# An attention and expert kernel whose instruction order is planned anew with other planner numbers

## The chip, the cores and the metric

The kernel runs on one core of one Trainium2 chip. The metric is the time of one execution on the device in microseconds (us); of several runs the median is taken. Engines: PE is the matrix engine, DVE the vector engine, ACT the scalar engine, POOL the GpSimd engine, and SP issues the transfers.

## The reference

```python
q_pool = q.reshape(B, H, S // 2, 2, D).mean(axis=3)          # B 4, H 8, S 1152, D 64
scores = np.matmul(q_pool, k.transpose(0, 1, 3, 2)) / np.sqrt(D)
scores = scores - np.max(scores, axis=-1, keepdims=True)
attn = np.exp(scores)
attn = attn / (np.sum(attn, axis=-1, keepdims=True) + 1e-09)
x = np.matmul(attn, v)                 # then to (2304, 512): heads side by side
h = x @ w_in                           # 512 -> 2048
g = np.where(h > 0.0, h, np.exp(np.minimum(h, 0.0)) - 1.0)
out = g @ w_out                        # 2048 -> 512
```

All inputs and the output are float32.

## The kernel before

The work is cut into tasks, each a few instructions of one engine. A planner, the class `Plan`, puts all tasks into one list when the program is built, and the engines get their instructions in the order of that list. Each engine works through its own queue in order; semaphores hold an instruction until what it reads is written. So nothing is decided on the chip: a task that stands too early in a queue makes its engine wait, and everything behind it too.

Attention. There are four units (one for each batch) of four head pairs each. A head pair has nine steps: eight of 128 pooled queries of one head, and one that holds the last 64 queries of both heads. That is 144 steps. A step is: `scores` on PE (L814, L819, L826: six matmuls, or twelve in the ninth step) into the one PSUM tile `s`; `biggest` on DVE (L832), which scales the scores into the SBUF tile `ep` and finds the row maximum; `expo` on ACT (L838) with the row sums; `recip` on DVE (L846 or L484, L847). As there is one tile `s`, the next step's scores wait until `biggest` has read the last ones. Then there are two ways, by `SPLIT`:
- in the six pairs marked f, `norm` (L850 on POOL, L853 on DVE, or L856 on ACT), transposes on PE (L906), copies out of PSUM (L916 on ACT or L919 on DVE), and float32 matmuls with v (`pv`, L938);
- in the ten pairs marked s, the probabilities are split into two float16 parts: `phi` (L874 on POOL or L877 on ACT) writes the high part `hb`, `plo` on DVE (L880) the rest; SP transposes both by DMA (L886), and PE multiplies them with a split v (`pv_split`, L950, 54 matmuls).

The result is copied to `x` (L959 on ACT, L963 or L965 on DVE). Ahead of each pair, q and k (and v where it is split) are loaded, summed (`q_sum`, L587 on POOL or DVE), scaled and split in `prep`, and turned by DMA.

Experts. When the x of a unit's first 256 tokens, and then of its last 320, is there, `experts` runs for that group: `m1` (L1053) into PSUM, `neg` (L1066) and `ex` (L1069) on ACT, `em` (L1074) on POOL, `join` (L1079) on DVE, then `gh` (L1093 on ACT or L1101 on POOL) and `gl` (L1097 on POOL or L1105 on DVE), which make the two float16 parts of g, then `m2` (L1124) and the way out (L1140 to L1150). The weights are unpacked on DVE (L696 to L700), and split by `w_hi` on ACT (L742) and `w_lo` (L745 on DVE, or L484 and L751 on POOL).

What sets the order: each task has a key, worked out from its place in the sum of steps, from the numbers in `CFG`, and from a number of its own in `NUDGE`. In `Plan.run` a modelled engine that is free takes, of the tasks whose predecessors are done by the model's durations (`add`'s second argument) and lags (`LAT`, `TAIL`, `SWITCH`), the one with the lowest key whose buffers are free. A task with more than one way (`ways`) goes to the engine at which the model thinks it is done sooner.

PE has its array whole ("full"), or cut into row or column halves ("row", "col"): `scores` ends in "row" (or starts in "col"), `pv`, `pv_split` and the 64 token blocks of `m2` are "col", the rest is "full". `modes` says so for each task.

Of the kernel before, what the change touches and what calls it, by code (L numbers as in the profile page):

```python
# [18 lines left out]
CFG = dict(  # L19
    LOADS=-2465884, WI0=-27823, WIT=30440, WO0=1311932, WOT=4783, T0=1480, T1=812, M0=21242,  # L20
    M1=58392, KS=5164412, KM=-16195, KE=597808, KH=-20226, KL=126077, KV=-42119, KN=-15967,
    KX=-43605, KO=-36554, PEN=-18129, W0L=26355, WIN=-42633, PD=3605, KS0=29075649, KM0=3580,
    KE0=43169, KH0=-7128, KL0=17190, KV0=-37362, KX0=35076, PLM0=0, NS0=36, PLM=0, M2=6438, DP=0,
    FK=0, PENW=-13844, PENH=10146, FL=2000, PH0=2, PH=1, KT=140078, KT0=-327, LV=15492, PENN=-24464,
    PENT=-48259, PLP=1, WLP=1, HIP=0, PA=9244, PB=93473, KA=40989, KB=-4257737, KC=34460,
)
# [46 lines left out]
    "turn0": -32562, "w_hii": -11591, "w_hio": 455, "w_loi": 299, "w_loo": -451, "wi_mino": -21137,  # L73
# [48 lines left out]
class Plan:  # L122
# [4 lines left out]
    TAIL = {"PE": 70.0, "DVE": 75.0, "ACT": 90.0, "POOL": 30.0, "DMA": 0.0}  # L127
# [12 lines left out]
    def add(self, eng, dur, key, emit, after=(), bufs=(), ways=(), modes=None):  # L140
        t = Task(eng, dur, key, emit, after, list(bufs))
        for e, d, f in ways:
            t.ways[e] = (d, f)
        for b in t.bufs:
            b.open += 1
        t.modes = modes or t.modes
        t.kind = emit.__name__ + self.at
        t.key += NUDGE.get(t.kind, 0)
        t.n = len(self.tasks)
        self.tasks.append(t)  # L150
        return t
# [25 lines left out]
    def run(self):  # L177
# [33 lines left out]
        def finish(t, at):  # L211
            t.end = at
            for b in t.bufs:
                b.open -= 1
            for kid in t.kids:
                kid.left -= 1
                kid.ready = max(kid.ready, at + self.TAIL[t.eng] + (30.0 if t.eng == "DMA" else self.LAT[kid.eng]))
                if kid.left == 0:
                    heapq.heappush(coming, (kid.ready, kid.n, kid))
# [5 lines left out]
        while done < len(self.tasks):  # L225
# [5 lines left out]
            while again:  # L231
                again = False
                for e in engines:
# [3 lines left out]
                    for _, _, t in wait[e]:  # L237
                        if e != t.eng:
# [12 lines left out]
                        if need is not None:  # L251
                            best = (t, need)
                            break
# [58 lines left out]
        self.span = now  # L312
# [12 lines left out]
def attention_moe_kernel(  # L325
# [67 lines left out]
    def dve(n):  # L393
        return Port(1.08 * n + 75.0)
# [4 lines left out]
    def pol(n):  # L399
        return 0.93 * n + 150.0  # L400

    def pol2(n):
        return Port(1.9 * n + 190.0)
# [87 lines left out]
    def across(src, n, key, after, bufs, take):  # L491
# [19 lines left out]
        return plan.add("DVE", Port(600.0), key, across_take, [t3], [xp] + bufs)  # L511


    def prep(pr, t0, t1):
# [40 lines left out]
        def halves(n, kh, kl, dst_h, dst_l, src, j, after, bufs):  # L555
# [3 lines left out]
            t = plan.add("DVE", dve(n), kl, f, [h], bufs, [("POOL", Port(pol(n), pol2(n)), g)] if CFG["PLP"] else [])  # L559
# [33 lines left out]
        qa = plan.add("DVE", dve(n), key[0], qadd(nc.vector), [tq], [q32], [("POOL", pol2(n), qadd(nc.gpsimd))])  # L593
# [602 lines left out]
```

## Time and profile before

| | us |
|---|---|
| median of 3 runs (841.58 to 841.83) | 841.66 |
| profiled execution, its own time | 844.75 |
| span of the profile | 843.0 |
| PE busy in the span | 750.6 (89%) |
| DVE busy | 682.2 (81%) |
| ACT busy | 594.3 (71%) |
| POOL busy | 329.3 (39%) |

The span runs from the first instruction to the last one's end; 1.75 us of the profiled execution lie around it. "Busy" is time in which the engine has at least one instruction at work. An idle time is named by what ended it: `PE s L814 <- DVE ep L832` is PE's wait to write scores until `biggest` on DVE has read the tile.

### The profile page before, as it was taken

Reading aid. Unit: us, or ns where it says so; the run is one execution under the profiler, and the core shown is the slowest. Engines: PE = TensorE matmul, PEld = TensorE weight load, DVE = VectorE, ACT = ScalarE, POOL = GpSimd, SP = SyncE. Lnnn points to the kernel's source line nnn. Section 1 sums busy time; section 2 is a strip of 40 time slices with the busy share of each in tenths; the row PEclk is TensorE's granted clock in tenths of the full one; section 3 lists DMA queues with packets and bytes.
Section 4 is the critical chain, followed back from the end, with each engine's and each line's share of the span. In section 5 each row is a group of like instructions: output and inputs, shape, how many; then the busy total and the mean of one; then the engine's idle time right before and its main releaser. Section 6 shows DMA issues by size and latency. Waiting matters only on the chain. (4 is left out here: it accounts for less than half of the span.)

```text
span 843.0 us, 19849 instructions
## 1 busy us (share of the span) xinstructions
PE 750.6 (89%) x7821; PEld 493.3 (59%) x7821; DVE 682.2 (81%) x1352; ACT 594.3 (71%) x1024; POOL 329.3 (39%) x318
## 2 busy tenths in 40 slices
PE   0178887899899999999978989999999999999997
PEld 0036665677655675576754557566746566586553
DVE  6889989999889789978987889979988799865140
ACT  3478989888887676767867678768878687655250
POOL 2412244326688216023643128315615365235120
PEclk9999999999999999999989999999999999999999
DMA  8954576546458329794979999999999989950000
GB/s 295 242 151 124 145 182 192 177 88 149 88 109 154 78 62 219 115 181 93 205 145 198 182 184 206 143 208 213 194 190 192 200 143 163 187 94 2 25 2 31
DMA packets 310813, 125.43 MB, mean 149 GB/s; under 512 B 272576, under 2 KB 291008, under 8 KB 310720
## 3 DMA queue, kind: packets, MB, share of 16 engines
q1 hardware_dynamic: 310720, 124.16, 71.9%
q8 instruction: 61, 1.00, 0.5%
q14 instruction: 32, 0.26, 0.1%
HBM read 45.09 MB, written 4.72 MB: 59 GB/s over the span
## 5 line engine op out<-in xcount | busy, mean ns | idle before, releaser
L838 ACT ACTIVATE ep<-ep,wk 128x1152 f32<-128x1152 f32 x144 | 180.3, 1252 | 73.2 <-DVE ep L832 54.0
L832 DVE TENSOR_SCALAR_CACHE_REDUCE ep<-s,sm 128x1152 f32<-128x1152 f32 x144 | 203.2, 1411 | 27.0 <-DMA pT<-ep 11.5
L1053 PE MATMUL r<-x,wi 128*128 128x256 f16 (+1 forms) x1536 | 201.6, 289 | 5.5 <-ACT x L959 2.4
L1053 PEld LDWEIGHTS <-wi 128*128 128x128 f16 x1536 | 148.6, 99 | 50.5 <-issue 11.4
L1124 PE MATMUL r<-wo,g 128*128 128x512 f16 (+1 forms) x864 | 174.0, 380 | 0.0
L880 DVE SCALAR_TENSOR_TENSOR ep<-ep,wk,hb 128x1152 f16<-128x1152 f32 x90 | 136.0, 1518 | 6.8 <-POOL hb L874 5.1
L814 PE MATMUL s<-kT,qT 128*128 128x512 f16 (+2 forms) x480 | 98.3, 338 | 34.0 <-DVE ep L832 28.3
L1124 PEld LDWEIGHTS <-g 128*128 128x128 f16 (+1 forms) x864 | 74.1, 100 | 83.8 <-issue 4.4
L874 POOL TENSOR_SCALAR hb<-ep,wk 128x1152 f16<-128x1152 f32 x41 | 56.0, 1365 | 149.8 <-DVE wk L847 72.6
L1074 POOL TENSOR_SCALAR tmp<-tmp,us 128x320 f32<-128x320 f32 (+1 forms) x96 | 78.2, 815 | 83.9 <-ACT tmp L1069 82.4
L850 POOL TENSOR_SCALAR ep<-ep,wk 128x1152 f32<-128x1152 f32 x34 | 42.4, 1247 | 114.7 <-DVE wk L847 30.6
L877 ACT ACTIVATE hb<-ep,wk 128x1152 f16<-128x1152 f32 x49 | 61.4, 1252 | 32.0 <-issue 8.2
L814 PEld LDWEIGHTS <-qT 128*128 128x128 f16 (+1 forms) x480 | 39.8, 102 | 74.3 <-issue 36.1
L1079 DVE SCALAR_TENSOR_TENSOR tmp<-r,wk,tmp 128x320 f32<-128x320 f32 (+1 forms) x96 | 57.1, 609 | 31.6 <-POOL tmp L1074 31.4
L950 PE MATMUL r<-pT,v 128*64 128x128 f16 (+1 forms) x2700 | 79.0, 215 | 2.9 <-DVE tmp L1079 1.0
L950 PEld LDWEIGHTS <-v 128*64 128x64 f16 x2700 | 71.9, 110 | 14.2 <-issue 12.5
L906 PE MATMUL r<-ident,ep 128*128 128x128 f32 x486 | 70.5, 292 | 3.2 <-ACT ep L856 2.4
L1097 POOL TENSOR_TENSOR g<-tmp,g 128x320 f16<-128x320 f32 (+1 forms) x49 | 55.8, 1143 | 25.1 <-ACT g L1093 24.1
L906 PEld LDWEIGHTS r<-ident,ep 128*128 128x128 f32 x486 | 55.1, 147 | 17.3 <-issue 9.9
L938 PE MATMUL r<-pT,v 128*64 128x128 f32 (+1 forms) x1080 | 61.0, 268 | 1.8 <-ACT pT L916 1.7
L1066 ACT ACTIVATE tmp<-r 128x320 f32<-128x320 f32 (+1 forms) x96 | 45.8, 480 | 23.0 <-PE r L1053 20.3
L916 ACT ACTIVATE pT<-r 128x384 f32<-128x384 f32 x125 | 53.7, 489 | 10.7 <-PE r L906 9.5
(119 smaller groups left out, 1001.5 us busy)
## 6 DMA issues: line engine op xcount, KB each, us to landing
k<-in_k_dram SPq DMA_DIRECT2D x16, 576.0 KB, 4.1
v<-in_v_dram SPq DMA_DIRECT2D x16, 576.0 KB, 4.7
q<-in_q_dram SPq DMA_DIRECT2D x32, 256.0 KB, 3.7
g<-in_moe_w_out_dram SPq DMA_DIRECT2D x14, 512.0 KB, 4.5
qT<-qT SPq DMA_DIRECT2D x48, 144.0 KB, 2.8
g<-in_moe_w_in_dram SPq DMA_DIRECT2D x13, 512.0 KB, 6.0
out_dram<-tmp SPq DMA_DIRECT2D x16, 256.0 KB, 2.7
h<-in_moe_w_in_dram SPq DMA_DIRECT2D x3, 512.0 KB, 3.8
```

The source lines that it names most:

```text
L814: nc.tensor.matmul(s.ap[rows, c, 0:n], pr.qT.ap[:, 0, j, rows], keys[h][c], start=True, stop=False, skip_group_check=True,)
L832: nc.vector.tensor_scalar(e_(), s.ap.rearrange("p a b -> p (a b)")[:, 0:S], pr.sm.ap[:, 12:13], None, op0=ALU.mult, op1=ALU.min, accum_out ...
L838: nc.scalar.activation(out=e_(), in_=e_(), func=AF.Exp, bias=nm.ap[:, 0:1], scale=-1.0, accum_out=nm.ap[:, 1:2],)
L877: nc.scalar.activation(out=hb.ap, in_=e_(), func=AF.Copy, scale=nm.ap[:, 1:2])
L880: nc.vector.scalar_tensor_tensor(out=e16(), in0=e_(), scalar=nm.ap[:, 1:2], in1=hb.ap, op0=ALU.mult, op1=ALU.subtract)
L906: nc.tensor.transpose(tp.ap[:, c * 128:(c + 1) * 128], e_()[:, (j + c) * 128:(j + c + 1) * 128], ident)
L938: nc.tensor.matmul(half(h), pr.v32.ap[:, h, order[c]], p, start=(c == 0), stop=(c == NCH - 1), skip_group_check=True,)
L950: nc.tensor.matmul(half(h), pr.v16.ap[:, h, order[c], e], p, start=(j + c == 0), stop=(j == 2 and c == NCH - 1), skip_group_check=True,)
L1053: nc.tensor.matmul(hp.ap[:, f * n:(f + 1) * n], w_in16[g][:, a, c, (f0 + f) * 128:(f0 + f + 1) * 128], x16.ap[:, e, c, g0:g0 + n], start=( ...
L1074: nc.gpsimd.tensor_scalar(en.ap[:, :m], en.ap[:, :m], -1.0, us.ap[:, 5:6], op0=ALU.add, op1=ALU.mult)
L1079: nc.vector.scalar_tensor_tensor(out=en.ap[:, :m], in0=hp.ap[:, :m], scalar=mf[:, g:g + 1], in1=en.ap[:, :m], op0=ALU.mult, op1=ALU.max,)
L1124: nc.tensor.matmul(op.ap[r0:r0 + tn, :], gt[qd].ap[:, a, fi, o:o + tn], w_out16(f // 2)[:, e, f % 2, :], start=(i < 128 // tn), stop=(i >= ...
```

## The change

The planner's model gets other numbers, two rules are added to it, and all of `CFG` and `NUDGE` is set anew. The tasks, their instructions and their buffers stay as they are; their order, and the engine of a task that has several ways, come out otherwise. Two lines stand for the tables:

```diff
-    LOADS=-2465884, WI0=-27823, WIT=30440, WO0=1311932, WOT=4783, T0=1480, T1=812, M0=21242,
+    MODE=-6415, LOADS=-529245, WI0=23907, WIT=50553, WO0=575761, WOT=14406, T0=13370, T1=5713,
...
-    TAIL = {"PE": 70.0, "DVE": 75.0, "ACT": 90.0, "POOL": 30.0, "DMA": 0.0}
+    TAIL = {"PE": 180.0, "DVE": 75.0, "ACT": 90.0, "POOL": 30.0, "DMA": 0.0}
...
-                kid.ready = max(kid.ready, at + self.TAIL[t.eng] + (30.0 if t.eng == "DMA" else self.LAT[kid.eng]))
+                kid.ready = max(kid.ready, at + t.lag + self.TAIL[t.eng] + (30.0 if t.eng == "DMA" else self.LAT[kid.eng]))
...
                     for _, _, t in wait[e]:
+                        if best is not None and t.key > best[0].key + CFG["MODE"]:
+                            break
+                        if best is not None and t.modes[0] != mode:
+                            continue
...
                             best = (t, need)
-                            break
+                            if e != "PE" or t.modes[0] == mode:
+                                break
...
-        return plan.add("DVE", Port(600.0), key, across_take, [t3], [xp] + bufs)
+        return plan.add("DVE", Port(250.0, 250.0, 200.0), key, across_take, [t3], [xp] + bufs)
...
-        qa = plan.add("DVE", dve(n), key[0], qadd(nc.vector), [tq], [q32], [("POOL", pol2(n), qadd(nc.gpsimd))])
+        qa = plan.add("DVE", dve(n), key[0], qadd(nc.vector), [tq], [q32], [("POOL", pol2(n) + 90.0, qadd(nc.gpsimd))])
...
-            ends.append(plan.add("DVE", Port(665.0), t0, w_lo, [h], bf, [("POOL", Port(pol(512), pol2(512)), w_lo_pool)] if CFG["WLP"] else []))
+            ends.append(plan.add("DVE", Port(665.0), t0, w_lo, [h], bf, [("POOL", Port(690.0, 1210.0), w_lo_pool)] if CFG["WLP"] else []))
...
-        tm = plan.add("DVE", 1345.0, t0 - K("KM", u), biggest, [ts_, pr.sc], [s, nm, ep, pr.sm])
+        tm = plan.add("DVE", 1345.0, t0 - K("KM", u), biggest, [ts_, pr.sc], [s, nm, ep, pr.sm], lag=45.0)
...
-            pr.pt.append(plan.add("DMA", Move(1400.0, 1100.0, True), t0 - CFG["KC"], ptr(0), [th], [hb, pT]))
+            pr.pt.append(plan.add("DMA", Move(1430.0, 1200.0, True), t0 - CFG["KC"], ptr(0), [th], [hb, pT]))
```

Where a task has several ways, the order counts these instructions (before, after): `gl` on DVE 42, 0 and on POOL 54, 96; `gh` on POOL 37, 4 and on ACT 59, 92; `phi` on POOL 41, 10 and on ACT 49, 80; the transposes' copies on DVE 37, 0 and on ACT 125, 162; the copies to `x` on ACT 49, 0 and on DVE 31, 80; `w_lo` on POOL 20, 2 and on DVE 12, 30; `q_sum` on POOL 10, 1 and on DVE 6, 15; `norm` on POOL 34, 34, on DVE 9, 16 and on ACT 11, 4. (The changed file has five lines more in front of these places: its L701 is L696 of before, and so on.)

Three places in the order. On DVE near the program's start, from the unpacking of the third w_in group's second half (tile `g4`) on (`sm` holds the first pair's scales, `wk` the weights' scales); before:

```order
L700 SCALAR_TENSOR_TENSOR g4_88<-g4_88,tmp3_135 128x512
L745 SCALAR_TENSOR_TENSOR wi1_62<-g0_80,wk_69,wi1_62 128x512
L502 TENSOR_REDUCE wk_69<-r0_152 2x1
L503 TENSOR_SCALAR wk_69<-ident_70,wk_69 2x2
L717 TENSOR_REDUCE wk_69<-wk_69 128x1
L609 TENSOR_SCALAR sm0_146<-r0_152 128x2
```

And now:

```order
L705 SCALAR_TENSOR_TENSOR g4_88<-g4_88,tmp3_135 128x512
L592 TENSOR_TENSOR q320_96<-q320_96 128x9x64
L750 SCALAR_TENSOR_TENSOR wi0_61<-h0_78,wk_69,wi0_61 128x512
L750 SCALAR_TENSOR_TENSOR wi0_61<-g0_80,wk_69,wi0_61 128x512
L722 TENSOR_REDUCE wk_69<-wk_69 128x1
L507 TENSOR_REDUCE wk_69<-r0_153 2x1
```

The sum of q and one more half of a weight split, which POOL did before, stand in DVE's queue ahead of the first pair's scales.

On POOL in the fourth unit's attention, beside the third unit's experts (`hb` is `phi`'s output, `tmp` the expert's, `g` and `h` the two parts of g); before:

```order
L1074 TENSOR_SCALAR tmp0_7658<-tmp0_7658,us0_6632 128x512
L874 TENSOR_SCALAR hb1_7698<-ep1_7665,wk_69 128x1152
L1097 TENSOR_TENSOR g4_7444<-tmp0_7658,g4_7444 128x2x256
L874 TENSOR_SCALAR hb1_7881<-ep0_7831,wk_69 128x1152
L1074 TENSOR_SCALAR tmp0_7874<-tmp0_7874,us0_6632 128x512
L1074 TENSOR_SCALAR tmp1_7940<-tmp1_7940,us0_6632 128x512
L1097 TENSOR_TENSOR g1_7795<-tmp0_7874,g1_7795 128x2x256
L1101 TENSOR_SCALAR g1_7795<-tmp1_7940 128x2x256
```

And now:

```order
L1079 TENSOR_SCALAR tmp0_7894<-tmp0_7894,us0_6773 128x512
L1079 TENSOR_SCALAR tmp2_7931<-tmp2_7931,us0_6773 128x512
L1079 TENSOR_SCALAR tmp1_7990<-tmp1_7990,us0_6773 128x512
L1102 TENSOR_TENSOR g1_7780<-tmp0_7894,g1_7780 128x2x256
L1102 TENSOR_TENSOR g2_7867<-tmp2_7931,g2_7867 128x2x256
L1102 TENSOR_TENSOR g2_7867<-tmp1_7990,g2_7867 128x2x256
L592 TENSOR_TENSOR q320_8051<-q320_8051 128x9x64
```

`phi` and `gh` are gone from this stretch of POOL's queue; they stand in ACT's.

On DVE from the last step's `biggest` on (`ep` probabilities, `x320` the attention's result, `tmp` the experts'); before:

```order
L832 TENSOR_SCALAR ep3_10223,wk_69<-s0_10196,sm0_8770 128x1152
L1143 SCALAR_TENSOR_TENSOR tmp0_10280<-r4_9843,us1_8251,tmp0_10280 64x512
L484 TENSOR_SCALAR wk_69<-wk_69 128x1
L847 RECIPROCAL wk_69<-wk_69 128x1
L880 SCALAR_TENSOR_TENSOR ep2_10092<-ep2_10092,wk_69,hb0_10173 128x1152
L963 TENSOR_SCALAR x320_8443<-r0_10225,sm0_8770 128x128
L991 TENSOR_REDUCE us1_10318<-x320_8443 128x1
L880 SCALAR_TENSOR_TENSOR ep0_10175<-ep0_10175,wk_69,hb1_10286 128x1152
L880 SCALAR_TENSOR_TENSOR ep3_10223<-ep3_10223,wk_69,hb0_10324 128x1152
```

And now:

```order
L837 TENSOR_SCALAR ep0_10406,wk_69<-s0_10333,sm1_8631 128x1152
L1084 SCALAR_TENSOR_TENSOR tmp1_10291<-r3_10250,wk_69,tmp1_10291 128x512
L968 TENSOR_SCALAR x320_8398<-r0_10349,sm1_8631 128x128
L885 SCALAR_TENSOR_TENSOR ep1_10324<-ep1_10324,wk_69,hb0_10408 128x1152
L489 TENSOR_SCALAR wk_69<-wk_69 128x1
L852 RECIPROCAL wk_69<-wk_69 128x1
L1084 SCALAR_TENSOR_TENSOR tmp2_10347<-r2_10296,wk_69,tmp2_10347 128x512
L885 SCALAR_TENSOR_TENSOR ep0_10406<-ep0_10406,wk_69,hb1_10477 128x1152
```

Three `plo` followed the last `biggest`, now two do, and the experts' joins of the fourth unit's first group stand between them. On PE, behind the last scores, 8 tasks `m1` of that group stood before, and 3 do now; five went in front of the last scores.

## Rows read from the trace of the kernel before

**Rows 1.** Busy time of each engine in four stretches, and their sum over the span.
```profile
0.00:42.30 42.30, 4.15 (x14) 2.42 (x15) 31.49 (x65) 16.23 (x32) 13.06 (x16) 1.00 0.91 269
42.30:174.00 131.70, 110.66 (x1040) 79.13 (x1040) 118.57 (x291) 112.15 (x222) 42.71 (x36) 0.96 0.58 162
174.00:735.60 561.60, 534.28 (x5959) 347.37 (x5958) 492.17 (x926) 422.59 (x693) 248.33 (x232) 0.99 0.85 159
735.60:838.30 102.70, 101.51 (x815) 64.40 (x812) 39.19 (x72) 42.64 (x78) 25.23 (x34) 1.00 0.16 34
...
sum 843.00, PE 750.59 PEld 493.31 DVE 682.16 ACT 594.30 POOL 329.32; mean PE 150.12 PEld 98.66 DVE 136.43 ACT 118.86 POOL 65.86
```

**Rows 2.** PE's waits by releaser: us in total, times, longest.
```profile
PE s L814 <- DVE ep L832: 28.3, 28, 2.5
```

**Rows 3.** Timeline of the start: start us, us, engine, line, operation, [idle before].
```profile
42.27 1.14 PE L814 MATMUL s<-kT,qT 128*128 128x512 f16 x3 [1.58 <-DMA qT<-qT]
```

**Rows 4.** Timeline of PE, two `pv_split` tasks and what starts behind them.
```profile
700.31 1.70 PE L950 MATMUL r<-pT,v 128*64 128x128 f16 x54
701.94 0.66 PE L814 MATMUL s<-kT,qT 128*128 128x512 f16 x3
...
713.32 1.70 PE L950 MATMUL r<-pT,v 128*64 128x128 f16 x54
714.85 1.46 PE L1124 MATMUL r<-wo,g 128*64 128x512 f16 x12
```

**Rows 5.** Groups of instructions, by form: busy us, mean ns | idle before.
```profile
L880 DVE SCALAR_TENSOR_TENSOR ep<-ep,wk,hb 128x1152 f16<-128x1152 f32 x90 | 136.0, 1518 | 6.8 <-POOL hb L874 5.1 <-ACT hb L877 1.4
L877 ACT ACTIVATE hb<-ep,wk 128x1152 f16<-128x1152 f32 x49 | 61.4, 1252 | 32.0 <-issue 8.2 <-DMA pT<-hb 4.9 <-ACT ep L838 4.0
L874 POOL TENSOR_SCALAR hb<-ep,wk 128x1152 f16<-128x1152 f32 x41 | 56.0, 1365 | 149.8 <-DVE wk L847 72.6 <-ACT kn L524 14.5 <-DMA pT<-hb 13.5
L916 ACT ACTIVATE pT<-r 128x384 f32<-128x384 f32 x125 | 53.7, 489 | 10.7 <-PE r L906 9.5
L1097 POOL TENSOR_TENSOR g<-tmp,g 128x320 f16<-128x320 f32 x31 | 31.5, 1021 | 11.3 <-ACT g L1093 10.6
L1105 DVE TENSOR_TENSOR g<-tmp,g 128x320 f16<-128x320 f32 x33 | 22.9, 700 | 8.2 <-ACT g L1093 6.3 <-POOL g L1101 1.5
L919 DVE COPY pT<-r 128x384 f32<-128x384 f32 x37 | 19.5, 551 | 2.4 <-PE r L906 2.3
L1101 POOL TENSOR_SCALAR g<-tmp 128x320 f16<-128x320 f32 x24 | 18.6, 779 | 13.5 <-DVE tmp L1079 13.4
L1093 ACT ACTIVATE g<-tmp 128x320 f16<-128x320 f32 x40 | 18.1, 460 | 6.0 <-DVE tmp L1079 5.9
L587 POOL TENSOR_TENSOR q<-q 128x576 f32<-128x576 f32 x10 | 17.5, 1751 | 39.9 <-DMA q<-in_q_dram 39.8
L751 POOL TENSOR_TENSOR wi<-g,wi 128x512 f16<-128x512 f32 x7 | 8.7, 1248 | 0.6
L959 ACT ACTIVATE x<-r,sm 128x128 f32<-128x128 f32 x25 | 8.6, 356 | 2.9 <-PE r L950 2.4 <-DVE x L1031 0.4
L745 DVE SCALAR_TENSOR_TENSOR wi<-g,wk,wi 128x512 f16<-128x512 f32 x6 | 5.7, 953 | 0.0
L587 DVE TENSOR_TENSOR q<-q 128x576 f32<-128x576 f32 x6 | 5.7, 952 | 7.8 <-DMA q<-in_q_dram 7.8
L963 DVE TENSOR_SCALAR x<-r,sm 128x128 f32<-128x128 f32 x15 | 5.0, 344 | 0.0
```

**Rows 6.** `plo` on DVE, duration in ns: shortest, median, longest.
```profile
L880 DVE SCALAR_TENSOR_TENSOR ep<-ep,wk,hb x90: 1397/1413/2379, 212.3 to 744.6; 128x1152 f16<-128x1152 f32 x90
```

**Rows 7.** Timeline of PE around the last `pv_split`.
```profile
735.59 0.68 PE L814 MATMUL s<-kT,qT 128*64 128x512 f16 x6
...
739.52 10.86 PE L1053 MATMUL r<-x,wi 128*128 128x256 f16 x96
...
753.16 1.04 PE L950 MATMUL r<-pT,v 128*64 128x64 f16 x54 [1.00 <-DVE tmp L1079]
```

More of the change, by code (lines that the diff above doesn't have):

```diff
@@ L19 @@
 CFG = dict(
-    LOADS=-2465884, WI0=-27823, WIT=30440, WO0=1311932, WOT=4783, T0=1480, T1=812, M0=21242,
[L21 to L25, printed above, removed]
+    MODE=-6415, LOADS=-529245, WI0=23907, WIT=50553, WO0=575761, WOT=14406, T0=13370, T1=5713,
+    M0=-6282, M1=116883, KS=188971, KM=-8340, KE=6072, KH=-5981, KL=2684, KV=-34675, KN=-61301,
+    KX=4466, KO=10885, PEN=2245, W0L=6942, WIN=-1811, PD=10220, KS0=1123529, KM0=29954, KE0=-23279,
+    KH0=-13414, KL0=-64965, KV0=-2050218, KX0=-11582, PLM0=0, NS0=36, PLM=0, M2=-1757, DP=0, FK=0,
+    PENW=1875, PENH=2978, FL=2000, PH0=2, PH=1, KT=1758, KT0=6138, LV=1212347, PENN=-9392,
+    PENT=18055, PLP=1, WLP=1, HIP=0, PA=-3857, PB=860938, KA=11746, KB=-4150, KC=-27088,
 )
 NUDGE = {
[43 rows of a table removed]
-    "turn0": -32562, "w_hii": -11591, "w_hio": 455, "w_loi": 299, "w_loo": -451, "wi_mino": -21137,
[8 rows of a table removed]
[43 rows of a table added]
+    "w_loi": 35013, "w_loo": 1247, "wi_mino": 26056, "wo_topo": -1688, "xb0": 26044, "xb1": -28175,
[7 rows of a table added]
 }
@@ L138, in buf, with add @@
         return Buf(self, tags)
-    def add(self, eng, dur, key, emit, after=(), bufs=(), ways=(), modes=None):
+    def add(self, eng, dur, key, emit, after=(), bufs=(), ways=(), modes=None, lag=0.0):
         t = Task(eng, dur, key, emit, after, list(bufs))
@@ L146, in add @@
         t.modes = modes or t.modes
+        t.lag = lag
         t.kind = emit.__name__ + self.at
@@ L311, in run @@
                 finish(t, at)
-        self.span = now
+        self.span = max([now] + [a for a, _, _ in landing])
         return order
@@ L558, in halves @@
             f, g = lo(dst_l, src, dst_h, j)
-            t = plan.add("DVE", dve(n), kl, f, [h], bufs, [("POOL", Port(pol(n), pol2(n)), g)] if CFG["PLP"] else [])
+            t = plan.add("DVE", Port(730.0, 730.0) if j == 1 else dve(n) + 35.0 * (j == 0), kl, f, [h], bufs, [("POOL", Port(pol(n), pol2(n)), g)] if CFG["PLP"] else [])
             t.pen = CFG["PENH"]
@@ L858, in attention @@
         n = 128 if st.h is not None else 64
-        ts_ = plan.add("PE", 850.0, t0 - K("KS", u), scores, pr.kdone + [pr.qs], [s, pr.kT, pr.qT],
+        ts_ = plan.add("PE", 866.0, t0 - K("KS", u), scores, pr.kdone + [pr.qs], [s, pr.kT, pr.qT],
                        modes=("full", "row") if st.h is not None else ("col", "both"))
-        tm = plan.add("DVE", 1345.0, t0 - K("KM", u), biggest, [ts_, pr.sc], [s, nm, ep, pr.sm])
+        tm = plan.add("DVE", 1345.0, t0 - K("KM", u), biggest, [ts_, pr.sc], [s, nm, ep, pr.sm], lag=45.0)
         te = plan.add("ACT", 1255.0, t0 - K("KE", u), expo, [tm], [nm, ep])
-        tr = plan.add("DVE", 250.0, t0 - K("KE", u), recip, [te], [nm])
+        tr = plan.add("DVE", 262.0, t0 - K("KE", u), recip, [te], [nm], lag=85.0)
         if not st.h:
@@ L894, in attention @@
             tl = plan.add("DVE", dve(S), t0 - CFG["KB"], plo, [th], [ep, nm, hb])
-            pr.pt.append(plan.add("DMA", Move(1400.0, 1100.0, True), t0 - CFG["KC"], ptr(0), [th], [hb, pT]))
-            pr.pt.append(plan.add("DMA", Move(1400.0, 1100.0, True), t0 - CFG["KC"], ptr(1), [tl], [ep, pT]))
+            pr.pt.append(plan.add("DMA", Move(1430.0, 1200.0, True), t0 - CFG["KC"], ptr(0), [th], [hb, pT]))
+            pr.pt.append(plan.add("DMA", Move(1430.0, 1200.0, True), t0 - CFG["KC"], ptr(1), [tl], [ep, pT]))
         else:
@@ L967, in attention @@
         vb = [pr.v16, pr.sm] if pr.split else [pr.v32]
-        tp = plan.add("PE", 27 * mm(n) if pr.split else 18 * (2.0 * n / 2.4 + 2.5), t0 + K("KV", u), pv_split if pr.split else pv,
+        tp = plan.add("PE", 27 * mm(n) if pr.split else 18 * (2.0 * n / 2.4 + 0.5), t0 + K("KV", u), pv_split if pr.split else pv,
                       list(pr.pt) + pr.vdone, [x, pT] + vb, modes=("col", "col"))
```

101 rows, old and new, of the table NUDGE are left out of this document.

## The prediction

> **What bounds the kernel now.** I read the table of stretches first, then PE's waits, then the start, the tilings' borders and the last steps on the timeline, and last the groups of the instructions that change their engine.
>
> The stretches are cut at the first scores (42.3 us), at 174 us, at the last scores (735.6) and at PE's last matmul (838.3) [rows 1]. PE is idle for 843.0 - 750.6 = 92.4 us of the span: 38.1 before the first scores, 131.7 - 110.7 = 21.0 up to 174 us, 561.6 - 534.3 = 27.3 up to the last scores, 1.2 up to its last matmul, and 4.7 us at the end, in which the last block is scaled and stored. So PE bounds the kernel from 174 us on (95% busy, and 99% behind the last scores), and nothing there is gained but by filling those 27.3 us. Between 42.3 and 174 us, where the pairs marked f run almost alone, DVE is busy for 118.6 of 131.7 us (90%), ACT for 85%, PE for 84%: there it is the chain between DVE and ACT that sets the pace. The reader is to see one more thing in the waits: of what PE waits for, the one tile `s` is the largest part, 28.3 us in 28 waits of 1.0 us on the mean, each for `biggest` on DVE [rows 2]. So DVE is late by a little, in 28 of 144 steps.
>
> **The change part by part.**
>
> The rule on tilings does nothing. `MODE` is -6415, and the tasks stand in the order of their keys, so the first look at a second task, whose key is never lower than the first one's, ends the search. Counted in the order, the borders at which PE changes its tiling are 262 before and 275 now, 13 more. The price of one: a `pv_split` that a half block of `m2` follows in the same tiling takes 714.85 - 713.32 = 1.53 us from start to start, and one that scores in the full array follow takes 701.94 - 700.31 = 1.63 us [rows 4]. That is 0.10 us for a border, 1.3 us in all, or nothing where PE would have waited there anyhow. I take +1.3. (The Trainium skill, page TensorEngine Tiling (Array Packing), section Key Properties, says that a change of tiling mode drains the engine and gives no price; by that rule the change makes PE's own work longer, as the two rows do.)
>
> The work that changes its engine, counts from the order, durations from [rows 5]:
> - DVE gives off 42 `gl` of 0.70 us (29.4) and 37 copies of 0.55 (20.4), and gets 9 `q_sum` of 0.95 (8.6), 18 `w_lo` of 0.95 (17.1), 49 copies to `x` of at most 0.34 (16.7) and 7 `norm`, which I price by the shortest `plo`, as wide as they are, at 1.4 (9.8) [rows 6]. That is 52.2 - 49.8 = +2.4 us at most.
> - ACT gets 31 `phi` of 1.25 (38.8), 37 copies of 0.49 (18.1) and 33 `gh` of 0.46 (15.2), and gives off 49 copies of 0.36 (17.4) and 7 `norm`, priced as `phi` (8.8): +45.9 us, from 594.3 to about 640.
> - POOL gives off 31 `phi` of 1.37 (42.3), 33 `gh` of 0.78 (25.7), 9 `q_sum` of 1.75 (15.8) and 18 `w_lo`, of whose two instructions the second alone takes 1.25 (22.5), and gets 42 `gl` of 1.02 (42.8): -63.5 us at least, 19% of its 329.3.
>
> What this is worth on DVE: its instructions get longer when POOL is at work. `plo` takes 1.397 us at its shortest, 1.413 in the median and up to 2.379 [rows 6], and 1.518 on the mean [rows 5], so 90 x 0.121 = 10.9 us are lost there. With 19% less of POOL, 2 us of that come back; all 10.9 would be the upper end. `w_lo` and `q_sum` on DVE (0.95 each) were themselves measured beside POOL's half of the same work, which is gone now, and most of them stand between the start and 174 us, where DVE sets the pace. I take -4 us for the stretch up to 174 us, with the ends -10.9 (all of the stretching of `plo`) and +2.4 (the moved work at its full price).
>
> (The Trainium skill, page SBUF — State Buffer, section Who interferes with whom, says that a DVE instruction with two SBUF inputs and a GpSimd instruction that reads SBUF exclude each other, so that the second one waits until the first has finished. The longest `plo`, which is 0.98 us over its shortest, agrees; that the median is within 0.02 us of the shortest, with POOL busy for 39% of the span, shows that it does not hit most of them.)
>
> The start. The first scores start at 42.27 us after a wait for the transfer that completes qT [rows 3]. In the new order the same four transposes and copies stand on SP with a third weight load in front of the last copy where there were two; DVE has one more `q_sum` and one more `w_lo` before the first pair's scales, but the unpacking before them is no longer beside POOL's `q_sum`. I take 0, from -2 (a DVE instruction or two) to +3 (the load, and a `q_sum` and two `w_lo` of 0.95 in the way). DVE has more of the weights done by then, which is part of the -4 above.
>
> The middle. Five `m1` tasks of 24 matmuls went from behind the last scores to places between scores. A task is 10.86 / 4 = 2.7 us [rows 7], so PE has 13.5 us less to do behind the last scores and 13.5 us more to put where it waits for `s`. If it falls into waits it is gained, if it stands beside them nothing is: the ends are -13.5 and 0. The waits are 28 and short, the tasks longer than the waits, so I take half, -7. The planner's longer lag behind PE works in the same direction: it no longer puts a task on ACT or DVE too early behind a matmul. What covers this is DVE at 88% and ACT at 75 + 6% in this stretch; without that cover the term is zero.
>
> The end. From the last scores to the last `pv_split` PE has 753.16 - 735.59 = 17.6 us now, and waits 1.0 us in it [rows 7]. With one `m1` less between them (three where four stood in front of that task) 17.6 - 1.0 - 2.7 = 13.9 us are left. In it the step must pass `biggest`, exp, `phi`, `plo` and the transposes. DVE has one `plo` fewer to do behind the last `biggest`, and two joins more in front of the last one. I take 0; if the chain needs as long as it did, 17.6 - 13.9 = 3.7 us of waiting come in, and at best the wait of 1.0 goes.
>
> Sum: 844.75 (the profiled execution: the span of 843.0 and 1.75 around it) + 1.3 - 4 + 0 - 7 + 0 = 835.05. The median of the runs, 841.66, is 3.1 below the profiled execution, so the forecast is **832.0 us**.
>
> **The rivals.**
>
> *ACT takes DVE's place (slower).* ACT is busy for (112.2 + 422.6) / 693.3 = 77% between the first and the last scores [rows 1], and 45.9 us more make 84%. Its queue is in order: a `phi` that waits for `recip` holds up the exp of the next step, and with it that step's `recip`, `plo` and transposes, and at last PE. For it: 31 more `phi` of 1.25 us stand there, and POOL, which had time for them (39% busy), is left idle. Against it: an exp is not needed by PE at once; the transposes and one or two other PE tasks lie between. It decides where ACT's share of a stretch passes the 90% at which DVE now sets the pace. If a quarter of the 38.8 us gets through to PE and the filling brings nothing: 841.66 + 1.3 - 4 + 9.7 = 848.7 us.
>
> *The idle time only moves (no change).* For it: PE's work is the same plus 1.3, and all of the gain is a share of waits that I chose. The weight half that went to DVE could eat the 4 us. Then it is 841.66 + 1.3 - 1 = 842 us.
>
> *POOL and DVE exclude each other for whole instructions (much faster).* The order has 67 POOL instructions fewer. If a DVE instruction had stood behind each for half of some 1.2 us (`phi`, 1.37, and `w_lo`, 1.25 [rows 5]), DVE gets 67 x 0.6 = 40 us back, and with half of it where DVE sets the pace, -20 takes the place of -4: 816 us. Against it stands the median of `plo`. (This is what the Trainium skill's page SBUF — State Buffer would make of the change.)
>
> **How the numbers follow.** The forecast has 0.57, with a range of its own from 824 to 840: the ends of its terms, of which not all come at once. The rival on ACT has 0.27, the one without change 0.08, the one on the port 0.08. The range must reach into the slower case and stops at 848, with half of it inside, and at 820, above the last rival; some 0.2 is left out. What differs by less than 0.2% (1.7 us) from 841.66 can't be told from no change. Faster: 0.57 + 0.08 = 0.65; same 0.08; slower 0.27.
>
> **What would show it.** In the changed kernel's profile PE's waits for `biggest` should be fewer than 28.3 us, PE's idle time between the first and the last scores below 48.3, and the last scores earlier relative to PE's last matmul: about 13 us less behind them. `plo`'s mean should fall from 1518 ns, POOL's busy time below 270 us, ACT's rise to about 640. The first scores should start between 40 and 45 us. I am wrong if ACT's waits on its own queue show up as PE waiting for pT, if the first scores come later than 45 us, or if PE's idle time in the middle is not less than before although the five tasks stand there.

## The result and the profile after

The changed kernel takes 826.9 us in the median of 4 runs (825.71 to 831.80), the kernel before 841.62 (838.54 to 841.83): 14.7 us less, a ratio of 0.9845 with a 95% interval of 0.9817 to 0.9873. The profiled execution took 825.71 us with a span of 823.9, so the two profiles differ by 19.1 us. That is 4.4 more than the medians: the profiled execution of before lies 3.1 us above its median, that of the changed kernel 1.2 below. Shares below are of the profiles.

The stretches, cut at the first scores, the 32nd scores, the last scores and PE's last matmul (the second border of [rows 1] lies 0.9 us behind the 32nd scores; columns: stretch, its length, busy us of PE, of its weight loads (PEld), of DVE, ACT and POOL, granted clock, DMA share, GB/s):

```profile
0.00:41.90 41.90, 5.14 (x16) 2.96 (x17) 31.60 (x80) 19.19 (x39) 0.70 (x6) 1.00 0.94 286
41.90:169.60 127.70, 105.35 (x1032) 75.55 (x1033) 119.37 (x288) 107.45 (x220) 32.46 (x26) 0.97 0.58 161
169.60:729.90 560.30, 544.27 (x6083) 357.17 (x6084) 479.41 (x943) 462.63 (x740) 173.64 (x177) 1.00 0.85 160
729.90:819.30 89.40, 88.69 (x694) 51.92 (x693) 23.45 (x47) 38.41 (x73) 31.72 (x43) 1.00 0.14 30
819.30:823.90 4.60, 0.00 (x0) 0.00 (x0) 0.74 (x1) 0.69 (x1) 0.00 (x0) 1.00 0.28 86
sum 823.90, PE 743.46 PEld 487.60 DVE 654.58 ACT 628.36 POOL 238.52; mean PE 148.69 PEld 97.52 DVE 130.92 ACT 125.67 POOL 47.70
```

The start is 0.4 us shorter. From the first scores to the last ones it is 688.0 us where it was 693.3, 5.3 less, although five more expert tasks stand there; behind the last scores PE has 89.4 us where it had 102.7, 13.3 less; the end is the same. That is the whole 19.1. Seen on PE, its busy time fell by 7.1 us (750.6 to 743.5, with the same 7821 matmuls) and its idle time by 12.0.

Where the five tasks went, on PE's timeline of the changed kernel (answers to [rows 7]; start us, us, engine, line, operation):

```profile
709.74 1.46 PE L1129 MATMUL r<-wo,g 128*64 128x512 f16 x12
711.13 5.42 PE L1058 MATMUL r<-x,wi 128*128 128x256 f16 x48
...
718.98 2.79 PE L1058 MATMUL r<-x,wi 128*128 128x256 f16 x24
...
723.54 2.79 PE L1058 MATMUL r<-x,wi 128*128 128x256 f16 x24
...
727.13 2.79 PE L1058 MATMUL r<-x,wi 128*128 128x256 f16 x24
729.86 0.68 PE L819 MATMUL s<-kT,qT 128*64 128x512 f16 x6
...
730.86 1.70 PE L955 MATMUL r<-pT,v 128*64 128x128 f16 x54
732.49 8.03 PE L1058 MATMUL r<-x,wi 128*128 128x256 f16 x72
...
743.28 1.02 PE L955 MATMUL r<-pT,v 128*64 128x64 f16 x54
```

The five tasks are the 120 matmuls of L1058 in front of the last scores; three more tasks follow behind these, and the last `pv_split` starts 13.4 us behind the last scores without a wait. Between 680 us and the last scores PE is not idle at all, and DVE is busy for 43.5 of the 49.9 us:

```profile
680.00:729.90 49.90, 49.90 (x615) 32.58 (x614) 43.45 (x82) 38.66 (x51) 8.85 (x10) 1.00 0.86 153
```

PE's largest wait, by releaser (us in total, times, longest), answers to [rows 2]; it is only 1.7 us shorter:

```profile
PE s L819 <- DVE ep L837: 26.6, 24, 5.0
```

The groups that answer to [rows 5 and 6] (busy us, mean ns | idle before; then shortest, median, longest in ns):

```profile
L885 DVE SCALAR_TENSOR_TENSOR ep<-ep,wk,hb 128x1152 f16<-128x1152 f32 x90 | 129.7, 1443 | 13.6 <-ACT hb L882 12.3 <-POOL hb L879 1.1
...
L592 DVE TENSOR_TENSOR q<-q 128x576 f32<-128x576 f32 x15 | 11.5, 768 | 13.2 <-DMA q<-in_q_dram 13.2
L750 DVE SCALAR_TENSOR_TENSOR wi<-g,wk,wi 128x512 f16<-128x512 f32 x13 | 10.3, 821 | 0.9 <-ACT wi L747 0.9
L701 DVE TENSOR_SCALAR tmp<-g 128x512 uint32<-128x512 uint32 x26 | 10.9, 418 | 1.8 <-DMA g<-in_moe_w_in_dram 1.8
L858 DVE TENSOR_SCALAR ep<-ep,wk 128x1152 f32<-128x1152 f32 x16 | 13.1, 820 | 0.5
...
L885 DVE SCALAR_TENSOR_TENSOR ep<-ep,wk,hb x90: 1398/1412/2036, 210.6 to 737.2; 128x1152 f16<-128x1152 f32 x90
```

`plo` is 75 ns shorter on the mean, `q_sum` on DVE takes 0.77 us where it took 0.95, `w_lo` 0.82 where it took 0.95. The unpacking (L701) takes 0.42 us where it took 0.64 in the kernel before:

```profile
L696 DVE TENSOR_SCALAR tmp<-g 128x512 uint32<-128x512 uint32 x27 | 17.3, 641 | 3.5 <-DMA g<-in_moe_w_in_dram 3.5
```

DVE's busy time fell by 27.6 us, to 654.6, although, on balance, it gave off 79 tasks and got 83. Some 11 us of this is the moved work at the durations that it has in the two traces: 50.0 us went (42 `gl`, 37 copies), and 38.7 us came. The rest is work that both kernels have on DVE and that got shorter: some 6 us each on `plo` and L701, and some 5 us on L705, the last step of the unpacking, and the small L508. Every `plo` that takes over 1.5 us, 21 before and 8 now, runs beside an instruction of POOL; none that runs without one takes over 1.42 us.

### The profile page after: what moved, and what is told of

It reads as the page before. It is cut to its first block, busy times and chain, and to the rows that moved or that the text cites. A ratio compares the mean times of both kernels' runs of the same rounds, so it can differ in the third digit from the quotient of the medians.

```text
span 823.9 us, 19802 instructions
## 1 busy us (share of the span) xinstructions
PE 743.5 (90%) x7821; PEld 487.6 (59%) x7821; DVE 654.6 (79%) x1356; ACT 628.4 (76%) x1069; POOL 238.5 (29%) x251
## 5 line engine op out<-in xcount | busy, mean ns | idle before, releaser
L1058 PE MATMUL r<-x,wi 128*128 128x256 f16 (+1 forms) x1536 | 199.8, 287 | 4.9 <-DVE x L968 1.9
L1129 PE MATMUL r<-wo,g 128*128 128x512 f16 (+1 forms) x864 | 176.2, 380 | 0.0
L1058 PEld LDWEIGHTS <-wi 128*128 128x128 f16 x1536 | 147.0, 98 | 49.1 <-issue 8.5
L885 DVE SCALAR_TENSOR_TENSOR ep<-ep,wk,hb 128x1152 f16<-128x1152 f32 x90 | 129.7, 1443 | 13.6 <-ACT hb L882 12.3
L882 ACT ACTIVATE hb<-ep,wk 128x1152 f16<-128x1152 f32 x80 | 99.9, 1249 | 36.8 <-DMA pT<-hb 15.9
L819 PE MATMUL s<-kT,qT 128*128 128x512 f16 (+2 forms) x480 | 96.2, 332 | 27.8 <-DVE ep L837 26.6
L1079 POOL TENSOR_SCALAR tmp<-tmp,us 128x320 f32<-128x320 f32 (+1 forms) x96 | 68.4, 715 | 180.3 <-ACT tmp L1074 164.1
L1102 POOL TENSOR_TENSOR g<-tmp,g 128x320 f16<-128x320 f32 (+1 forms) x88 | 90.2, 1033 | 91.5 <-ACT g L1098 90.7
L855 POOL TENSOR_SCALAR ep<-ep,wk 128x1152 f32<-128x1152 f32 x34 | 44.4, 1305 | 188.1 <-DVE wk L852 85.1
L921 ACT ACTIVATE pT<-r 128x384 f32<-128x384 f32 x162 | 68.4, 493 | 16.5 <-PE r L911 15.4
L955 PEld LDWEIGHTS <-v 128*64 128x64 f16 x2700 | 71.3, 110 | 13.3 <-issue 12.7
L911 PEld LDWEIGHTS r<-ident,ep 128*128 128x128 f32 x486 | 53.5, 143 | 17.0 <-issue 7.8
L1074 ACT ACTIVATE tmp<-tmp,us 128x320 f32<-128x320 f32 (+1 forms) x96 | 57.4, 610 | 1.2
```

Source lines behind the costliest of these rows:

```text
L819: nc.tensor.matmul(s.ap[rows, c, 0:n], pr.qT.ap[:, 0, j, rows], keys[h][c], start=True, stop=False, skip_group_check=True,)
L882: nc.scalar.activation(out=hb.ap, in_=e_(), func=AF.Copy, scale=nm.ap[:, 1:2])
L885: nc.vector.scalar_tensor_tensor(out=e16(), in0=e_(), scalar=nm.ap[:, 1:2], in1=hb.ap, op0=ALU.mult, op1=ALU.subtract)
L911: nc.tensor.transpose(tp.ap[:, c * 128:(c + 1) * 128], e_()[:, (j + c) * 128:(j + c + 1) * 128], ident)
L921: nc.scalar.activation(out=dst(j), in_=tp.ap[:, 0:384], func=AF.Copy)
L955: nc.tensor.matmul(half(h), pr.v16.ap[:, h, order[c], e], p, start=(j + c == 0), stop=(j == 2 and c == NCH - 1), skip_group_check=True,)
```

## The experiments

**Engines or order.** The tasks of the two kernels are the same 2878, so the two parts of the change can be exchanged: a table gives tasks to the engine that they have in the other kernel, at their own place in the list.

```diff
+        to = {n: e for e, ns in ENGINE.items() for n in ns}
         for t in self.run():
+            if t.n in to:
+                t.emit = t.ways[to[t.n]][1]
             for b in t.bufs:
```

The kernel before with all 259 engines of the changed one:

> The kernel before, its order of tasks kept, but each of the 259 tasks that stand on another engine in the changed kernel is given to that engine (at its own place in the list). If the gain of 14.7 us comes from the choice of engines (POOL's 90 us less beside DVE), it should be near 832 us and DVE's busy time should fall from 682 to about 656 us. If it comes from the order, it stays at 841.6 us within 3, although DVE's busy time falls. If the order of before was made for its engines, the new queues make waits and it is slower, 850 us or more.

Measured: 862.75 us (861.26 to 865.17), ratio to before 1.0239 (1.0206 to 1.0273). The changed kernel with the engines of before:

> The changed kernel, its order of tasks kept, but the same 259 tasks are given back to the engine that they have in the kernel before. If the gain comes from the choice of engines, it goes: 838 to 842 us, with DVE's busy time back near 680 us. If it comes from the order alone, 827 to 830 us. If the order was made for its engines, more than 842 us.

Measured: 859.69 us (858.45 to 862.83), ratio 1.0195 (1.0160 to 1.0230). Neither the engines nor the order bring anything alone; each is 2% slower than the kernel before. (22 of the 259 tasks are `norm`; they were moved in these two kernels only, not by themselves.) That the engines alone shorten DVE's work is seen on the page of the first of these two kernels:

```profile
PE 755.2 (88%) x7821; PEld 495.2 (58%) x7821; DVE 655.9 (76%) x1356; ACT 634.1 (74%) x1069; POOL 236.9 (28%) x251
```

DVE is busy for 655.9 us, as in the changed kernel (654.6) and 26 us less than before, and still the time is 20 us longer than that of the kernel before. DVE's sum is not what the time hangs on.

**One group of tasks at a time, back in the changed kernel.**

> The changed kernel with only w_lo (18) and q_sum (9) given back to POOL as before. If the port between POOL and DVE is what counted, DVE's unpacking and splits get longer again by some 10 us near the start, and the time is 830 to 834 us. If these only moved work between two engines with time to spare, 827 us within 2.

Measured: 834.45 us (831.32 to 837.88), ratio 0.9898 (0.9865 to 0.9931), 7.5 us over the changed kernel in the medians.

> The changed kernel with only phi on the engines of before (38 go back to POOL, 7 to ACT). If ACT's queue is what the change had to pay (the slower rival), ACT is relieved by 39 us and the time falls below 826 us. If POOL's phi, 1.37 us beside DVE, stretches DVE again and comes later than the order reckons with, the time is 832 to 840 us, and plo's mean goes from 1443 ns back towards 1518.

Measured: 837.77 us (836.01 to 840.41), ratio 0.9930 (0.9908 to 0.9953), 10.9 us over in the medians. `plo` goes back to a mean of 1532 ns:

```profile
L900 DVE SCALAR_TENSOR_TENSOR ep<-ep,wk,hb 128x1152 f16<-128x1152 f32 x90 | 137.8, 1532 | 13.8 <-POOL hb L894 7.3 <-ACT hb L897 6.1
```

> The changed kernel with only gh and gl on the engines of before (35 gh to POOL, 2 to ACT, 42 gl to DVE). DVE has 30 us more to do in the stretch where the experts run beside attention. If DVE sets the pace there, 838 to 846 us. If PE's own work does, and DVE has room, 827 to 831 us.

Measured: 829.97 us (828.46 to 830.77), ratio 0.9841 (0.9810 to 0.9873). That is 3.1 us over in the medians, but the ratio is that of the changed kernel (0.9845): no cost is shown here, although DVE has 19.7 us more to do:

```profile
PE 742.5 (90%) x7821; PEld 487.2 (59%) x7821; DVE 674.3 (81%) x1398; ACT 617.3 (75%) x1036; POOL 226.9 (27%) x242
```

> The changed kernel with only the copies out of PSUM on the engines of before (37 of the transposes' copies to DVE, 49 copies to x to ACT). Neither touches POOL, and DVE's sum changes by 3 us only. If the gain is the port between POOL and DVE, this changes nothing: 827 us within 3. If any task on another engine than the one the order was made for costs a wait, it is slower by 5 us or more, as the whole set was.

Measured: 840.52 us (839.61 to 844.07), ratio 0.9986 (0.9967 to 1.0005), 13.6 us over in the medians, without a task moved to or from POOL.

**The same groups, moved in the kernel before.** If a group's new engine were better by itself, it would be faster here.

> The kernel before, its order kept, with only w_lo (18) and q_sum (9) taken from POOL to DVE, as the changed kernel has them. If freeing the port between POOL and DVE is good by itself, it is faster than 841.6 us by 2 to 8 us. If what counts is that order and engine fit, it is slower by about as much as the same tasks cost when they went back in the changed kernel (7.5 us): 845 to 850 us.

Measured: 850.20 us (849.26 to 850.80) against 840.77, ratio 1.0120 (1.0092 to 1.0149).

> The kernel before, its order kept, with only phi on the engines of the changed kernel (38 from POOL to ACT, 7 the other way). If phi is better on ACT by itself, 835 to 840 us. If order and engine must fit, about 11 us slower than before, as the same tasks cost in the changed kernel: 850 to 855 us.

Measured: 854.86 us (852.24 to 855.26), ratio 1.0170 (1.0138 to 1.0202). `plo`'s mean stays where it was although POOL has 31 `phi` fewer:

```profile
L895 DVE SCALAR_TENSOR_TENSOR ep<-ep,wk,hb 128x1152 f16<-128x1152 f32 x90 | 136.0, 1518 | 6.7 <-ACT hb L892 5.7 <-POOL hb L889 0.6
```

> The kernel before, its order kept, with only gl on POOL (42 from DVE) and gh on ACT (35 from POOL). DVE is relieved by 29 us. If DVE's sum sets the pace beside the experts, 832 to 838 us. If only the fit of order and engine counts, 842 to 846 us, as these tasks cost 3 us in the changed kernel.

Measured: 843.84 us (839.83 to 845.77), ratio 1.0035 (1.0012 to 1.0058).

> The kernel before, its order kept, with only the copies out of PSUM on the engines of the changed kernel (37 of the transposes' copies on ACT, 49 copies to x on DVE). If the changed kernel's choice is better by itself in the stretch up to 170 us, where DVE sets the pace, 836 to 840 us. If order and engine must fit, about 14 us slower, as the same copies cost in the changed kernel: 850 to 856 us.

Measured: 849.64 us (847.88 to 851.07), ratio 1.0114 (1.0082 to 1.0145).

Three of the four groups cost time in both directions when they are moved off the engine for which the order was made: `w_lo` and `q_sum` 7.5 and 9.4 us, `phi` 10.9 and 14.1, the copies 13.6 and 8.9. (The first of each pair compares the medians of two series; by their ratios to the kernel before it is 4.5, 7.2 and 11.9 us.) `gl` and `gh` cost 3.1 us in the order of before, and nothing that is shown in the new one. So no group is faster on its new engine by itself; what a choice is worth depends on the order that was made with it. Through which waits a moved task costs time was not followed, and it was not tried whether any other disturbance of these orders, of the same size, would cost as much.

**The five tasks.** Without any task on another engine, the planner alone is told that the last unit's first `m1` come behind the last scores:

```diff
+        plan.last = ts_
...
-                    t1_ = plan.add("PE", per * 12 * mm(n), at, m1_all, [xready] + w_done[0][g] + late, [hp, x16, G])
+                    t1_ = plan.add("PE", per * 12 * mm(n), at, m1_all, [xready] + w_done[0][g] + late + ([plan.last] if u.i == 3 and gi == 0 else []), [hp, x16, G])
```

> The changed kernel, with one dependency more for the planner alone: the eight m1 tasks of the last unit's first group come behind the last scores, where before had them. PE's order is the same up to its 572nd task of 628. If the five m1 tasks fill waits between scores (the term of 7 us in the prediction), the waits for biggest between 700 us and the last scores come back and the time is 832 to 836 us. If DVE and ACT keep up without the filling, the last scores come 13 us earlier and the time stays at 827 us within 2.

Measured: 841.26 us (838.65 to 846.97, 10 runs), ratio to before 1.0001 (0.9975 to 1.0027): 14.4 us over the changed kernel in the medians (13.1 by the ratios), as slow as before, and slower than either case that was expected. Its timeline of PE before the last scores, and its waits for `biggest` over the whole program:

```profile
714.54 2.75 PE L1130 MATMUL r<-wo,g 128*64 128x512 f16 x24
718.84 0.66 PE L819 MATMUL s<-kT,qT 128*128 128x512 f16 x3 [1.54 <-DVE ep L837]
...
723.05 0.65 PE L819 MATMUL s<-kT,qT 128*128 128x512 f16 x3 [1.54 <-DVE ep L837]
...
725.11 1.04 PE L956 MATMUL r<-pT,v 128*64 128x64 f16 x54 [1.04 <-DVE x L969]
729.94 1.14 PE L819 MATMUL s<-kT,qT 128*128 128x512 f16 x3 [3.78 <-DVE ep L837]
...
733.46 1.17 PE L819 MATMUL s<-kT,qT 128*64 128x512 f16 x6 [1.73 <-DVE ep L837]
```

```profile
PE s L819 <- DVE ep L837: 36.1, 30, 5.0
```

The orders part at the block of `m2` that starts at 714.54 us here and at 709.74 in the changed kernel. Up to there the queues of all engines hold the same instructions in the same order, so the 4.8 us by which this execution is behind are a difference between two executions, and nothing that the tasks did. From there to the last scores it is 18.9 us here and 20.1 in the changed kernel. So the five tasks, 13.5 us of PE's work, made this stretch only 1.2 us longer (1.3 us of `m2` stand here in their stead). Waits of 9.6 us stand where the tasks stood, and the rest went into slow matmuls (below). From the last scores to the end it is 108.1 us here and 94.0 in the changed kernel. Of the 17.7 us between the two profiles, 12.9 thus arise behind the place where the orders part.

## Why the prediction was right

The forecast was 832.0 us, 9.6 below before; measured are 14.7. The direction and the places of the gain were right; the term of the middle was less than half of what came, and PE's shorter busy time had no term.

- *The rule on tilings.* With the rule taken out, the planner puts out the same order on every engine; it did nothing, as said.
- *The moved work.* POOL 238.5 us (below 270 was said), ACT 628.4 (about 640), `plo` shorter (1443 ns). But DVE fell by 27.6 us, where I had the moved work at up to +2.4 and the stretching at -10.9 at the best. The moved work is about -11: I had priced `norm` at 1.4 us, and it takes 0.82 (0.90 before); `w_lo` and `q_sum` are shorter than the 0.95 that I took. And I had counted the stretching of `plo` only, where the unpacking got shorter too.
- *Up to 174 us, -4.* The sign was right, and the size is a little smaller. It has to be read where PE has done the same work, as the orders put other tasks of PE between the scores. From the program's start to the 32nd, 33rd and 35th scores (columns as above), in the kernel before:

```profile
0.00:173.13 173.13, 113.94 (x1047) 81.16 (x1048) 149.29 (x351) 127.51 (x252) 55.72 (x52) 0.97 0.66 188
0.00:177.34 177.34, 118.14 (x1098) 84.46 (x1099) 153.33 (x364) 131.72 (x259) 56.99 (x53) 0.97 0.67 187
0.00:189.72 189.72, 129.33 (x1215) 93.38 (x1216) 165.36 (x390) 142.95 (x281) 59.45 (x55) 0.97 0.64 178
```

  And in the changed one:

```profile
0.00:169.59 169.59, 110.48 (x1048) 78.50 (x1049) 150.97 (x367) 126.62 (x257) 33.16 (x32) 0.98 0.67 192
0.00:178.35 178.35, 117.46 (x1122) 84.10 (x1122) 159.26 (x388) 135.32 (x274) 35.91 (x34) 0.98 0.66 189
0.00:187.71 187.71, 126.26 (x1215) 90.69 (x1216) 167.44 (x409) 143.19 (x289) 40.31 (x37) 0.98 0.64 181
```

  At the 32nd scores PE has done 1047 and 1048 matmuls, and the changed kernel is 3.2 us earlier, counted from the first scores; at the 35th, with 1215 each, 1.6 us. The 33rd scores alone would say 1.4 us later, but there PE has 24 matmuls more behind it. DVE has 16 instructions more done by the 32nd scores and is busy for only 1.7 us more. That the relief of DVE made this gain is not shown; the exchange kernels show that over the whole program the relief without its order is worth less than nothing.
- *The middle, -7 of at most -13.5.* The mechanism was right in the main, and the term was mis-sized: behind the last scores PE has 13.3 us less, and from the 32nd scores to the last ones the time is 2.2 us shorter, not longer, which makes 15.5. PE's idle time from the second border to the last scores took up most of the tasks: it fell from 27.3 to 16.0 us. The kernel with the tasks put back has 12.9 us of its loss behind the place where the orders part. I had argued that the tasks (2.7 us) are longer than the waits (1.0 us on the mean over the whole program) and took half. That step failed, because the tasks do not fall into the waits that I had counted. In the kernel before, PE waits for `biggest` for hardly anything between 680 us and the last scores:

```profile
PE s L814 <- DVE ep L832: 1.9, 2, 1.6
```

  There PE has 645 matmuls in the 55.6 us up to the last scores; the new order without the five tasks has 572 in 53.5 us. The waits in which the tasks stand are those that this kernel shows, 9.6 us in all and up to 3.8 us each, and most of them end with `biggest`: there DVE sets the pace, not PE.
- *The start and the end, 0 each.* 0.4 us and 0.1 us shorter. The last `pv_split` came 13.4 us behind the last scores, as worked out (13.9), and did not wait.
- *The rival on ACT.* ACT's share between the first and the last scores is (107.5 + 462.6) / 688.0 = 83%, as worked out, and the changed kernel is not slower for it: `phi` back on POOL costs 10.9 us in the medians. In the order of before, though, `phi` on ACT costs 14.1 us; whether ACT's queue is the cause there, as the rival has it, was not followed.
- *The rival on the port.* By this rival DVE was to get 40 us back; it got 27.6, of which 11 are the moved work. That half of it is gained is refuted by the kernel before with the new engines: DVE is relieved by 26 us there and the time is 20 us longer.

What stays open is the 5.3 us from the first to the last scores. PE's idle time there fell from 48.3 to 22.4 + 16.0 = 38.4 us, and its busy time rose by only 4.7 us although five tasks of 13.5 us came in: its other work is 8.8 us shorter, where I had added 1.3 us for the borders (the slow matmuls are fewer, see the last section). Which of the planner's numbers brought this is not shown. Engines and order can't be judged alone, as shown, and the tables of one planner with the model of the other give no complete order.

## What to carry to other kernels

Where an engine bounds the whole but waits briefly in one stretch, look in the stretch behind it for work of that engine that could already run. Here 13.5 us of such work cost 1.2 us, as another engine set the pace. Count the waits in the order that the work goes into, not in the one that it comes from. A choice of engine and an order made for it are one thing: price neither by the sums of busy time, and do not judge both by a test of one alone. A kernel with one dependency more in its planner is a cheap test of what one move in an order is worth.

## What the runs showed of the hardware that was not expected

PE's clock. The columns are the stretch, its length, PE's busy time, the granted clock (1.00 is 2.4 GHz, 0.50 is 1.2), DMA. In the kernel before:

```profile
73.00:80.00 7.00, 5.00 (x30) 0.76 0.57 167
138.00:142.00 4.00, 3.67 (x16) 0.57 0.47 129
158.00:162.00 4.00, 4.00 (x31) 0.57 0.45 153
226.00:231.00 5.00, 4.38 (x20) 0.66 0.00 0
431.00:439.00 8.00, 6.51 (x31) 0.57 0.56 104
493.00:497.00 4.00, 2.98 (x32) 1.00 0.99 192
```

In the changed kernel the second to the fifth of these times are at full clock; the first has less clock than before, and the last one, which was at full clock, has not. (The same time is not the same place in the program.)

```profile
73.00:80.00 7.00, 5.29 (x27) 0.52 0.60 171
138.00:142.00 4.00, 2.90 (x28) 1.00 0.42 131
158.00:162.00 4.00, 2.54 (x18) 1.00 0.22 86
226.00:231.00 5.00, 5.00 (x27) 1.00 1.06 226
431.00:439.00 8.00, 8.00 (x101) 1.00 0.84 166
493.00:497.00 4.00, 4.00 (x38) 0.57 1.33 166
```

Over the span the granted clock is 0.987 before and 0.994 now. By an estimate from these two figures that is 843.0 x 0.013 / 0.5 = 22 us and 823.9 x 0.006 / 0.5 = 10 us at 1.2 GHz: 12 us fewer, in which PE does half of what it could, so up to 6 us of the gain. The clock alone does not give the time: the kernel with `phi` back on POOL has a clock of 0.994 to 0.997 in its runs (the changed one 0.994 to 1.000), and is slower by 10.9 us in the medians.

In the kernel with the five tasks put back the clock falls behind the waits (columns as in the first table):

```profile
718.00:724.00 6.00, 3.63 (x66) 2.44 (x66) 4.41 (x8) 3.64 (x5) 0.00 (x0) 1.00 0.83 153
724.00:729.00 5.00, 1.12 (x56) 1.03 (x54) 3.96 (x7) 2.72 (x4) 0.00 (x0) 1.00 0.75 103
729.00:736.00 7.00, 4.33 (x34) 2.20 (x36) 5.97 (x11) 4.69 (x6) 0.00 (x0) 0.52 0.87 169
```

PE is busy for 4.8 of the 11 us up to 729, at full clock, and the next 7 us are at 0.52. Its scores at 723.05 take 0.65 us for three matmuls, those at 729.94, after a wait of 3.78 us, 1.14. There the waits of PE cost more than their length; the prediction had no term for that.
